# A fused convolution and SiLU MLP: first step as one whole chunk, second chunk by DMA transpose, output sums beside their own step

## The chip, the cores and the metric

The kernel runs on one core of one Trainium2 chip. The metric is device time in microseconds (us). A timed run and the profiled span differ by about 1.5 us (696.66 and 695.1 us for the kernel before); decompositions below use the span. In the profile, PE is the matmul engine (TensorE) and PEld its weight loads, DVE is VectorE, ACT is ScalarE, POOL is GpSimd and SP is the queue that issues most DMAs.

## The reference, cut to what matters

```python
def _attn_ref(x, weight):                    # x: 8 x 4096 x 192, weight: 8 heads x 7 taps
    w = exp(weight - max); w = w / sum(w)    # softmax over the 7 taps
    # causal depthwise convolution: out[s] = sum_k w[head, k] * x[s - 6 + k]
    ...
def _moe_ref(x, w_in, w_out, beta):          # 32768 x 192 -> 2048 -> 192
    h = x @ w_in
    g = h * sigmoid(beta * h)
    return (g @ w_out).astype(np.float32)
```

## The kernel before

Tokens are worked in chunks of 512, for two halves of the batch at once. A step takes one chunk through 16 groups. Group `u` does six input matmuls (`hidden`: 64 rows, 512 columns, two of them at a time on the two halves of the rows) and one activation of 128x1024, and beside them 16 output matmuls (`output`, 64 rows, 192 columns) of the **previous** step. Meanwhile VectorE convolves a later chunk by 21 "taps" (7 taps times 3 slices of the 192 channels), and evicts four output accumulators.

The first chunk is different: its convolution is done on PE with diagonal matrices, in two halves of 256 tokens, so that the first input matmul can start early. The second chunk comes in by a casting DMA and is transposed on PE. All later chunks are cast into HBM by GpSimd DMAs and then transposed by a DMA on the SP queue.

```python
    steps = [(0, 0, TOK // 2), (0, TOK // 2, TOK // 2)]        # chunk 0 in two halves
    steps += [(ch, 0, TOK) for ch in range(1, N_CH)]
    ...
    def xpose(ch):                                             # DMA transpose, SP queue
        nc.sync.dma_start_transpose(new_xt(ch)[:, :, r0:], xd[r0:].rearrange(...))
    ...
            if fc == NF - 1 and (b == 1 or single):            # eviction: copy, then add
                    nc.vector.tensor_copy(dst, po[:, 0, cols])
                nc.vector.tensor_tensor(dst, po[:, 1, cols], dst, ALU.add)
                store(s, h, q, n_q, osb)
    ...
    pops = {1: 12, 2: 26}
    for s in range(N_ST + 1):
        if s + 2 < N_ST:
            queue.extend(conv_ops(s + 2))      # step s + 2 reads chunk s + 1
        for u in range(NF):
            if s < N_ST:
                hidden(s, u)
            if s > 0:
                output(s - 1, u)               # the step before
            ...
            for _ in range(pops_u):            # 24 taps a step
                if queue:
                    queue.popleft()()
            if u == 0 and s + 4 < N_CH:
                cast(s + 4)
            if u == 1 and s + 2 < N_CH:
                xpose(s + 2)                   # convolved one step later
```

## Time and profile before

| Kernel before | us |
|---|---|
| time, median of 3 runs | 696.66 |
| profiled span | 695.1 |
| start of the first activation | 11.84 |
| last activation of chunk 1 ends | 53.5 |
| each of the next 30 steps (the first of them 20.63) | 20.92 |
| from the last activation to the end of the span | 14.3 |

The step times here and below are read from the trace: the end of the 16th activation of a step, less that of the step before.

The page of the kernel before, its fourth part (the chain of waits that ended last, by engine and by line):

```profile
PE 96%; DVE 3%; ACT 0%; issue 0%
PE po L442 48%; PE ph L395 46%; DVE ct L378 2%; PE ph L256 0%; DVE w_in_s L172 0%; DVE ct L376 0%; PE ph L205 0%; PE po L209 0%; PE po L243 0%; ACT g L402 0%; PE po L256 0%; DVE xt L346 0%; DVE osb L457 0%; DVE ct L327 0%; ACT xt_145 L269 0%
```

Nearly the whole chain is PE at work: L395 are the input and L442 the output matmuls. The groups of the same page (busy time, mean ns of one, then idle time of that engine just before them and who ended it):

```profile
L402 ACT ACTIVATE g<-ph,beta 128x1024 bf16<-128x1024 f32 (+1 forms) x528 | 572.7, 1090 | 96.7 <-PE ph L395 92.6
...
L378 DVE SCALAR_TENSOR_TENSOR ct<-xt,cw,ct 128x512 bf16<-128x512 bf16 x558 | 379.4, 745 | 0.0
...
L456 DVE COPY osb<-po 128x384 f32<-128x384 f32 x127 | 70.8, 558 | 126.9 <-PE po L442 120.7
L457 DVE TENSOR_TENSOR osb<-po,osb 128x384 f32<-128x384 f32 x129 | 71.5, 555 | 6.0 <-ACT osb L454 1.6
...
L376 DVE TENSOR_SCALAR ct<-xt,cw 128x512 bf16<-128x512 bf16 x93 | 29.5, 372 | 0.0
```

The copies (L456) stand 120.7 us in all for PE to finish an accumulator: VectorE is ahead of PE. And the first tap of a chunk (L376), which needs the DMA transpose, never waits: its idle time is 0.0. VectorE and the SP queue of the kernel before around 305 us (start, us, engine, line, operation, count, and in brackets the idle time before it):

```profile
303.79 0.56 DVE L456 COPY osb<-po 128x384 f32<-128x384 f32 x1 [0.77 <-PE po L442]
304.38 0.56 DVE L457 TENSOR_TENSOR osb<-po,osb 128x384 f32<-128x384 f32 x1
304.85 0.87 DVE L376 TENSOR_SCALAR ct<-xt,cw 128x512 bf16<-128x512 bf16 x3
```

```profile
304.96 0.37 SPq L417 DMA_DIRECT2D out_dram<-osb  x1
305.44 1.48 SPq L104 DMA_TRANSPOSE xt<-xd  x1
```

A copy and an add take 1.06 us from the start of the copy to the start of the next tap. The transpose is issued behind the store, at 305.44, while VectorE has been convolving another chunk, already in place, since 304.85. That the transpose lands some 5 us later hurts nobody.

### The profile page before, as it was taken

How to read it: one execution, taken by the hardware profiler on the slowest of the kernel's cores; microseconds unless marked ns; L12 is line 12 of the kernel's file. 1: busy time of each engine (PE TensorE's matmuls, PEld its weight loads, DVE VectorE, ACT ScalarE, POOL GpSimd, SP SyncE). 2: the span in 40 equal slices, each digit the busy share in tenths (PEclk: the TensorE clock that was granted, in tenths of full speed). 3: DMA queues.
4: the chain of work that ended last, by engine and by line, in shares of the span. 5: the costliest groups of instructions: out<-in, count | busy, mean ns of one | idle time of the engine just before them, and what ended most of it. 6: DMA issues, size and time to landing. Idle time of an engine off the chain costs nothing.

```text
span 695.1 us, 24865 instructions
## 1 busy us (share of the span) xinstructions
PE 687.6 (99%) x11467; PEld 526.6 (76%) x11467; DVE 551.4 (79%) x938; ACT 580.0 (83%) x546; POOL 70.0 (10%) x83
## 2 busy tenths in 40 slices
PE   9999999999999999999999999999999999999997
PEld 6867777777777777777777777777777777777777
DVE  5999998998777987777987777987778987777222
ACT  6898888888888888888888888888888888888881
POOL 7934455000000000000000000000000000000000
PEclk9999999999999999999999999999999999999999
DMA  9999999922232022222023222032222122211012
GB/s 193 144 159 159 168 177 171 123 63 70 54 65 71 27 68 72 47 70 70 26 71 70 49 70 70 25 71 70 48 71 55 40 70 71 48 48 48 25 48 70
DMA packets 181497, 54.57 MB, mean 79 GB/s; under 512 B 146432, under 2 KB 181072, under 8 KB 181392
## 3 DMA queue, kind: packets, MB, share of 16 engines
q0 software_dynamic: 98048, 14.89, 29.8%
q1 hardware_dynamic: 83296, 38.09, 23.9%
q8 instruction: 89, 1.46, 0.9%
q14 instruction: 16, 0.13, 0.1%
q10 hardware_dynamic: 48, 0.01, 0.0%
HBM read 28.98 MB, written 37.29 MB: 95 GB/s over the span
## 4 chain that ended last, share of the span: by engine, by line
PE 96%; DVE 3%; ACT 0%; issue 0%
PE po L442 48%; PE ph L395 46%; DVE ct L378 2%; PE ph L256 0%; DVE w_in_s L172 0%; DVE ct L376 0%; PE ph L205 0%; PE po L209 0%; PE po L243 0%; ACT g L402 0%; PE po L256 0%; DVE xt L346 0%; DVE osb L457 0%; DVE ct L327 0%; ACT xt_145 L269 0%
## 5 line engine op out<-in xcount | busy, mean ns | idle before, releaser
L402 ACT ACTIVATE g<-ph,beta 128x1024 bf16<-128x1024 f32 (+1 forms) x528 | 572.7, 1090 | 96.7 <-PE ph L395 92.6
L442 PEld LDWEIGHTS <-g 64*128 64x128 bf16 x8192 | 369.2, 94 | 101.9
L442 PE MATMUL po<-w_out_s,g 64*128 64x192 bf16 x8192 | 429.8, 243 | 0.0
L395 PE MATMUL ph<-ct,w_in_s 64*128 64x512 bf16 (+1 forms) x3168 | 426.2, 370 | 2.0 <-ACT g L402 1.1
L378 DVE SCALAR_TENSOR_TENSOR ct<-xt,cw,ct 128x512 bf16<-128x512 bf16 x558 | 379.4, 745 | 0.0
L395 PEld LDWEIGHTS <-w_in_s 64*128 64x128 bf16 x3168 | 162.5, 94 | 56.4 <-issue 2.9
L456 DVE COPY osb<-po 128x384 f32<-128x384 f32 x127 | 70.8, 558 | 126.9 <-PE po L442 120.7
L457 DVE TENSOR_TENSOR osb<-po,osb 128x384 f32<-128x384 f32 x129 | 71.5, 555 | 6.0 <-ACT osb L454 1.6
L95 POOL DMA_DIRECT2D xd<-in_x_dram x60 | 54.4, 909 | 46.1 <-DMA xd<-in_x_dram 42.3
L376 DVE TENSOR_SCALAR ct<-xt,cw 128x512 bf16<-128x512 bf16 x93 | 29.5, 372 | 0.0
L454 ACT COPY osb<-po 128x192 f32<-128x192 f32 x2 | 0.6, 320 | 9.9 <-PE po L442 9.9
L352 POOL TENSOR_TENSOR w_out_s<-w_out_raw,beta_r 128x768 bf16<-128x768 f32 x4 | 6.2, 1568 | 2.5 <-DMA w_out_raw<-in_moe_w_out_dram 2.5
L205 PE MATMUL ph<-zeros 128*128 128x512 bf16 x7 | 3.5, 623 | 1.3 <-DVE warm L129 1.3
L172 DVE COPY w_in_s<-w_in_s 64x1536 bf16<-64x1536 bf16 x4 | 4.4, 1121 | 0.1
L256 PE MATMUL po<-xt_145,diag 128*128 128x256 f32 x28 | 4.4, 296 | 0.0
L256 PEld LDWEIGHTS po<-xt_145,diag 128*128 128x128 f32 x28 | 3.6, 189 | 0.7 <-issue 0.6
L256 PEld LDWEIGHTS ph<-xt_145,diag 128*128 128x128 f32 x14 | 3.1, 327 | 0.6 <-ACT xt_145 L269 0.6
L256 PE MATMUL ph<-xt_145,diag 128*128 128x256 f32 x14 | 3.4, 427 | 0.1
L185 POOL DMA_DIRECT2D w_out_raw<-in_moe_w_out_dram x4 | 3.1, 771 | 0.3 <-DMA x1b<-in_x_dram 0.3
L295 ACT ACTIVATE ct<-po,rn 128x256 bf16<-128x256 f32 x1 | 0.5, 475 | 2.6 <-PE po L256 2.6
L165 POOL DMA_DIRECT2D w_in_s<-in_moe_w_in_dram x4 | 2.7, 669 | 0.0
L205 PEld LDWEIGHTS <-zeros 128*128 128x128 bf16 x7 | 0.8, 126 | 2.3 <-DVE warm L129 1.3
(51 smaller groups left out, 28.1 us busy)
## 6 DMA issues: line engine op xcount, KB each, us to landing
out_dram<-osb SPq DMA_DIRECT2D x60, 384.0 KB, 3.1
xd<-in_x_dram POOLq DMA_DIRECT2D x54, 198.0 KB, 14.5
w_out_raw<-in_moe_w_out_dram POOLq DMA_DIRECT2D x4, 384.0 KB, 9.4
out_dram<-osb SPq DMA_DIRECT2D x7, 192.0 KB, 3.7
xd<-in_x_dram POOLq DMA_DIRECT2D x6, 192.0 KB, 13.7
x_83<-in_x_dram SPq DMA_DIRECT2D x4, 192.0 KB, 2.9
w_in_s<-in_moe_w_in_dram POOLq DMA_DIRECT2D x4, 192.0 KB, 7.7
xt<-xd SPq DMA_TRANSPOSE x30, 5.1
```

Of the source, the lines that this page charges most:

```text
L95: nc.gpsimd.dma_start(out=xd[r0:, :, h, :], in_=x_v[p, t0:t1, h, :].rearrange("t (c d) -> t c d", c=NG),)
L172: nc.vector.tensor_copy(w_in_s[DG : 2 * DG, :, cols], w_in_s[0:DG, :, cols])
L205: nc.tensor.matmul(pf[:, 0, :], zeros[:, 0:128], zeros, start=True, stop=True)
L256: nc.tensor.matmul(pv, diag[:, c, k, :], xt0[:, c, o : o + n], start=(k == 0), stop=(k == K - 1),)
L352: nc.gpsimd.tensor_tensor(w_out_s[:, c0 : c0 + n, :], w_out_raw[:, c0 : c0 + n, :], beta_r[:, c0 : c0 + n].unsqueeze(2).to_broadcast((128, ...
L376: nc.vector.tensor_scalar_mul(dst, src, scalar)
L378: nc.vector.scalar_tensor_tensor(out=dst, in0=src, scalar=scalar, in1=dst, op0=ALU.mult, op1=ALU.add)
L395: nc.tensor.matmul(ph[:, h, 0:n], w_in_s[rows, j, cols], cts[s][rows, j, 0:n], start=(j == 0), stop=(j == NG - 1),)
L402: nc.scalar.activation(gs[s][:, fc, :, 0:n], ph[:, :, 0:n], AF.Silu, scale=beta[:, fc : fc + 1])
L442: nc.tensor.matmul(po[:, r, b * D : (b + 1) * D], g[rows, fc, h, q * BLK : (q + 1) * BLK], w_out_s[rows, fc, :], start=(fc == 0), stop=(fc ...
L456: nc.vector.tensor_copy(dst, po[:, 0, cols])
L457: nc.vector.tensor_tensor(dst, po[:, 1, cols], dst, ALU.add)
```

## The change

Its intent: spend the lead-in better. The whole first chunk is convolved by diagonals at N=512 and becomes one full step; the second chunk comes in by a DMA transpose instead of 48 small PE transposes (one third of its convolution is still done on PE, beside step 0); and the output sums of a step start in two accumulators while that step's own activations still run, so that fewer are left over at the end. Evictions become one reduce over the two halves of an accumulator. The core of the diff:

```diff
-    steps = [(0, 0, TOK // 2), (0, TOK // 2, TOK // 2)]
-    steps += [(ch, 0, TOK) for ch in range(1, N_CH)]
-    N_ST = len(steps)
+    N_ST = N_CH
 ... (psum_o with two buffers becomes psum_a and psum_b with one each)
+    cast(1)
+    for i in range(1, NW):
+        load_w_in(i)
+    cast(2)
+    cast(3)
+    xpose(1)                                   # on the SP queue ...
+    for i in range(1, NW):
+        load_w_out(i)                          # ... ahead of these weights
 ...
+    for c in range(NG):                        # chunk 0 whole: 21 matmuls at N=512
+        for k in range(K):
+            diag_tap(c, k, xt0[:, c], pv)
 ...
+                nc.vector.tensor_reduce(       # eviction
+                    dst,
+                    self.po[:, :, 0 : nb * D].rearrange("p r n -> p n r"),
+                    axis=mybir.AxisListType.X,
+                    op=ALU.add,
+                )
 ...
+    LAG = 2                                    # own step's sums, two groups behind
 ...
+    first_work = {
+        1: lambda: (copy_w_in(1), scale_w_out(1)),
 ...
+            output(s, u, 8, "a" if s == 0 and u <= CONV1[-1] else "ab")
 ...
             if u == 1 and s + 2 < N_CH:
                 xpose(s + 2)
+                queue.extend(conv_ops(s + 2, 0))   # step s + 2 now reads chunk s + 2
```

## The prediction

> **What bounds it now.** PE. The chain of waits that ended last is 96% PE; the page shows PE busy 99%, granted clock full. In the timeline a full step (16 times 6 input and 16 output matmuls) repeats every 16 x 1.308 = 20.92 us. VectorE was busy 89% from 100 to 200. So 32 x 20.92 = 669 us is GEMM at full rate; the other 26 us of the 695.1 us span are lead-in (first input matmul at 10.88), first half steps, and tail (last input matmul 679.5).
>
> **What the change does to start and end.**
> - Lead-in grows: 21 diagonal matmuls at N=512 instead of 256 (157 ns each when warm, 240 before). I estimate the first activation near 15 us instead of 11.84.
> - Step 0 becomes one full step, bound by activations: 16 x 1.09 = 17.4 us, with outputs hidden beside it. DMA transposes land 10.4 us after issue here, so chunk 1 arrives near its use (18 to 20 us). Step 0 ends at 33 to 34 us.
> - Then 31 steps x 20.92 = 648.6. The order of instructions shows 144 output matmuls after the last hidden one instead of 256: 5.9 us instead of 10.5. With 4.1 us of last eviction and store: 692, a gain of 3 us if nothing else changed.
> - Evictions: copy + add (1.06 us a pair) become one reduce over 768 PSUM elements. A 128x768 PSUM read by tensor_tensor took 0.94 us; the Trainium skill, "VectorE: DVE Perf Modes", section on the perf-mode tier table, gives tensor_reduce 1x only. I expect about 0.93 us.
>
> **What I think decides it: a new loop through VectorE.** Before, the taps run in a step read a chunk transposed one step earlier. Now chunk s+2 is transposed and convolved in the same step. The transpose stands on the SP queue behind the two stores of the pair of reduces at the start of the step, and the taps follow it. A backlog of 19 taps hides this at first, but 24 are popped and 21 pushed per step: 16, 13, 10, 7, 4, 1, 0. From step 8 the order of VectorE is: two reduces, 3 taps, reduce, 6 taps, reduce, 12 taps, two reduces. The cycle: store and queue 0.5 + transpose to landing 5.0 (quiet stage) + 3 first taps at 0.29 + 18 taps at 0.675 back to back + 4 reduces at about 0.92 + waits 0.2 = about 22.5 us, against PE's 20.92. PE then waits for the delayed reduce at the start of each step: 22 steps (8 to 29) x 1.6 = 35 us, plus 6 us in steps 4 to 7 (contended landings). Steps 30 and 31 convolve nothing: full rate.
>
> **Predicted:** span about 732, time 734 us; 8 in 10 between 712 and 752. Faster 0.03, same 0.11, slower 0.86.
>
> **Signs.** Right: VectorE idle about 5 us per step at the first tap, released by the transpose's landing; PE waiting 1 to 2.5 us per step on the reduce at the first output matmul of the second input group; step period about 22.5 us from step 8, 20.9 in the last two; first steps near 21; tail shorter by 4 us; first activation near 15.
>
> **What would make it wrong.** A reduce costlier than 1.1 us (two PSUM banks, strided) adds 4x the excess per step; landings under 3.5 us would close the loop within PE's time and leave about 692 to 697.

## The result

| | before | after |
|---|---|---|
| time, median of 4 runs each (us) | 696.66 | 720.38 |
| ratio, 95% interval | | 1.0342 (1.0328 to 1.0357) |
| profiled span | 695.1 | 719.7 |
| start of the first activation | 11.84 | 16.95 |
| from there to the end of chunk 1's last activation | 41.7 | 51.2 (30.15 + 21.08) |
| the 30 steps after that | 627.3 | 641.0 |
| from the last activation to the end of the span | 14.3 | 10.5 |

A ratio is the mean time of one kernel's runs over that of the other's of the same rounds, so it is not quite the ratio of the medians quoted. Executions over 1.5% slower than the fastest of the same kernel are left out of the means. The change makes the kernel 3.4% slower. The rows of the table add up: +5.1, +9.6, +13.7 and -3.8 make the 24.6 us by which the span grew.

The page of the changed kernel, the same part as shown for before:

```profile
PE 43%; DVE 27%; DMA 24%; issue 4%; POOL 1%; SPq 1%; ACT 0%; POOLq 0%
PE ph L363 20%; DVE ct L347 18%; DMA xd<-in_x_dram 14%; PE pa L393 12%; PE pb L393 10%; DMA xt<-xd 9%; DVE osb L412 7%; DVE ct L345 1%; POOL xd L104 1%; SPq L420 1%; ACT g L371 0%; POOL sel L158 0%; POOL sel L167 0%; POOL sel L156 0%; DVE osb L410 0%
```

The chain is no longer PE alone: 27% of it is VectorE and 24% DMA, among them 9% for the transposes (`DMA xt<-xd`). A chain that goes from DMA to VectorE to PE and round again is what a loop of waits looks like on a page. Not every wait on the chain is a cost: most of the 14% for the casts (`DMA xd<-in_x_dram`) lies between 46 and 113 us, and the steps there take 21.1 to 21.2 us, no more than later steps without any stall. The groups of the page:

```profile
L347 DVE SCALAR_TENSOR_TENSOR ct<-xt,cw,ct 128x512 bf16<-128x512 bf16 x552 | 371.7, 745 | 0.0
L393 PE MATMUL pa<-w_out_s,g 64*128 64x192 bf16 x4128 | 240.5, 243 | 9.3 <-DVE osb L412 7.5
...
L345 DVE TENSOR_SCALAR ct<-xt,cw 128x512 bf16<-128x512 bf16 x92 | 27.5, 351 | 119.2 <-DMA xt<-xd 119.2
L412 DVE TENSOR_REDUCE osb<-pa 128x384 f32<-128x768 f32 x64 | 61.0, 954 | 42.0 <-PE pa L393 41.9
...
L256 PE MATMUL pb<-xt,diag 128*128 128x512 f32 x7 | 4.1, 582 | 8.2 <-DVE xt L327 8.2
...
L291 DVE TENSOR_TENSOR w_out_s<-w_out_raw,beta_r 128x768 bf16<-128x768 f32 x4 | 3.8, 952 | 8.3 <-DMA w_out_raw<-in_moe_w_out_dram 8.3
```

The first taps (L345) now stand 119.2 us for the transposes, where before they stood for nothing; output matmuls stand 7.5 us for the reduces; and the diagonal matmul of chunk 1 (L256 into `pb`) stands 8.2 us, VectorE 8.3 us for output weights (L291). These are three different places. First the regular steps, VectorE of the changed kernel over one cycle:

```profile
303.83 0.95 DVE L412 TENSOR_REDUCE osb<-pa 128x384 f32<-128x768 f32 x1
304.70 0.95 DVE L412 TENSOR_REDUCE osb<-pb 128x384 f32<-128x768 f32 x1
310.80 0.88 DVE L345 TENSOR_SCALAR ct<-xt,cw 128x512 bf16<-128x512 bf16 x3 [5.15 <-DMA xt<-xd]
311.59 0.95 DVE L412 TENSOR_REDUCE osb<-pa 128x384 f32<-128x768 f32 x1
312.46 4.06 DVE L347 SCALAR_TENSOR_TENSOR ct<-xt,cw,ct 128x512 bf16<-128x512 bf16 x6
316.43 0.95 DVE L412 TENSOR_REDUCE osb<-pb 128x384 f32<-128x768 f32 x1
317.30 8.03 DVE L347 SCALAR_TENSOR_TENSOR ct<-xt,cw,ct 128x512 bf16<-128x512 bf16 x12
325.25 0.95 DVE L412 TENSOR_REDUCE osb<-pa 128x384 f32<-128x768 f32 x1
326.12 0.94 DVE L412 TENSOR_REDUCE osb<-pb 128x384 f32<-128x768 f32 x1
```

its SP queue in the same stretch:

```profile
304.81 1.24 SPq L420 DMA_DIRECT2D out_dram<-osb  x2
306.15 1.50 SPq L113 DMA_TRANSPOSE xt<-xd  x1
```

and PE at the start of it:

```profile
303.31 0.83 PE L363 MATMUL ph<-ct,w_in_s 64*128 64x512 bf16 x6
304.84 0.83 PE L393 MATMUL pa<-w_out_s,g 64*128 64x192 bf16 x16 [0.69 <-DVE osb L412]
```

After the second reduce VectorE has nothing to do until 310.80, 5.15 us, because the transpose of the chunk it has to convolve in this step was issued only at 306.15, behind the two stores of the two reduces. VectorE then does its taps and reduces without a pause, the next pair of reduces comes late, and PE stands for the first reduce of the pair (0.69 us here, 0.32 us at the end of this cycle). From the second reduce of one pair to that of the next the cycle is 0.95 + 5.15 + 0.79 + 0.87 + 3.97 + 0.87 + 7.95 + 0.87 = 21.42 us, against 20.92 us that PE needs for a step.

That explains steps of 21.4 to 22 us. But the trace also holds many steps in which PE shows no idle time over 0.15 us and which still take 21.17 us, not 20.92. The times of the activations put the extra 0.247 us (1.555 instead of 1.308 us) into one place, from the second to the third activation of the step. PE and VectorE there, in a step of 21.17 us:

```profile
367.02 0.51 PE L393 MATMUL pa<-w_out_s,g 64*128 64x192 bf16 x8
367.36 0.51 PE L393 MATMUL pb<-w_out_s,g 64*128 64x192 bf16 x8
367.69 0.83 PE L363 MATMUL ph<-ct,w_in_s 64*128 64x512 bf16 x6
368.58 0.84 PE L393 MATMUL pa<-w_out_s,g 64*128 64x192 bf16 x16
```

```profile
367.57 0.96 DVE L412 TENSOR_REDUCE osb<-pa 128x384 f32<-128x768 f32 x1 [0.38 <-PE pa L393]
```

Accumulator `pa` gets its last matmuls at 367.02, `pb` its last at 367.36: both end in the same group. The next output matmuls need `pa` again at once. PE has only the eight matmuls of `pb` and the next six input matmuls to do in between, 0.33 + 0.65 = 0.98 us, while the reduce starts at 367.57 and ends at 368.53, and `pa` is used again at 368.58: the next group starts 0.24 us after the input matmuls that precede it would have let it (367.69 + 0.65 = 368.34). Every step pays this, a new handoff wait that the prediction's arithmetic left out.

The third place is step 0. The windows view of the changed kernel (busy us of each engine in each stretch, number of instructions, then granted clock PEclk, DMA share, GB/s):

```profile
20.00:25.00 5.00, 0.94 (x10) 0.22 (x5) 0.00 (x0) 2.12 (x3) 1.45 (x3) 0.85 1.55 181
25.00:30.00 5.00, 0.88 (x5) 0.44 (x7) 2.21 (x4) 0.00 (x0) 1.35 (x2) 0.50 1.50 230
30.00:35.00 5.00, 5.00 (x32) 1.89 (x28) 4.93 (x8) 2.09 (x2) 0.80 (x1) 0.62 1.83 147
```

PE stands from 20.97 to 29.12 us, VectorE from 19.45 to 27.76 and ScalarE from 22.12 to 31.67; for 5.6 us all three stand at once. When PE returns, the granted clock is 0.50, and it stays there until 33.8 us (0.62 is the mean of the third stretch). What they stood for, in the timeline of the same kernel:

```profile
14.77 2.91 SPq L113 DMA_TRANSPOSE xt<-xd  x1
...
17.74 4.08 SPq L132 DMA_DIRECT2D w_out_raw<-in_moe_w_out_dram  x3
...
27.76 0.96 DVE L291 TENSOR_TENSOR w_out_s<-w_out_raw,beta_r 128x768 bf16<-128x768 f32 x1 [8.32 <-DMA w_out_raw<-in_moe_w_out_dram]
28.64 0.43 DVE L327 CAST xt<-xt 128x528 fp32r<-128x528 bf16 x1
...
29.12 0.80 PE L256 MATMUL pb<-xt,diag 128*128 128x512 f32 x1 [8.15 <-DVE xt L327]
```

Chunk 1 was cast into HBM by 14.70 us, its transpose issued at 14.77 and landed at 24.34. The output weights stand behind it on the SP queue, were issued from 17.74 and the first of them landed at 27.74. VectorE, in order, has to scale these weights (L291) before it may copy chunk 1 (L327), and PE, in order, has the first diagonal matmul of chunk 1 (L256) ahead of the rest of step 0.

### The profile page after: what moved, and what is told of

It is laid out like the page before. It is cut to its first block, busy times and chain, and to the rows that moved or that the text cites. A ratio compares the mean times of both kernels' runs of the same rounds, so it can differ in the third digit from the quotient of the medians.

```text
span 719.7 us, 24619 instructions
## 1 busy us (share of the span) xinstructions
PE 696.2 (97%) x11325; PEld 521.7 (72%) x11325; DVE 522.7 (73%) x807; ACT 578.7 (80%) x532; POOL 60.4 (8%) x74
## 4 chain that ended last, share of the span: by engine, by line
PE 43%; DVE 27%; DMA 24%; issue 4%; POOL 1%; SPq 1%; ACT 0%; POOLq 0%
PE ph L363 20%; DVE ct L347 18%; DMA xd<-in_x_dram 14%; PE pa L393 12%; PE pb L393 10%; DMA xt<-xd 9%; DVE osb L412 7%; DVE ct L345 1%; POOL xd L104 1%; SPq L420 1%; ACT g L371 0%; POOL sel L158 0%; POOL sel L167 0%; POOL sel L156 0%; DVE osb L410 0%
## 5 line engine op out<-in xcount | busy, mean ns | idle before, releaser
L371 ACT ACTIVATE g<-ph,beta 128x1024 bf16<-128x1024 f32 x512 | 570.2, 1115 | 122.5 <-PE ph L363 118.5
L393 PEld LDWEIGHTS <-g 64*128 64x128 bf16 x8192 | 368.0, 94 | 121.1 <-issue 20.5
L363 PE MATMUL ph<-ct,w_in_s 64*128 64x512 bf16 x3072 | 424.5, 377 | 0.3 <-ACT g L371 0.2
L347 DVE SCALAR_TENSOR_TENSOR ct<-xt,cw,ct 128x512 bf16<-128x512 bf16 x552 | 371.7, 745 | 0.0
L393 PE MATMUL pa<-w_out_s,g 64*128 64x192 bf16 x4128 | 240.5, 243 | 9.3 <-DVE osb L412 7.5
L393 PE MATMUL pb<-w_out_s,g 64*128 64x192 bf16 x4064 | 224.5, 243 | 0.0
L345 DVE TENSOR_SCALAR ct<-xt,cw 128x512 bf16<-128x512 bf16 x92 | 27.5, 351 | 119.2 <-DMA xt<-xd 119.2
L412 DVE TENSOR_REDUCE osb<-pa 128x384 f32<-128x768 f32 x64 | 61.0, 954 | 42.0 <-PE pa L393 41.9
L412 DVE TENSOR_REDUCE osb<-pb 128x384 f32<-128x768 f32 x63 | 59.8, 950 | 10.9 <-PE pb L393 10.9
L256 PE MATMUL pb<-xt,diag 128*128 128x512 f32 x7 | 4.1, 582 | 8.2 <-DVE xt L327 8.2
L256 PEld LDWEIGHTS pb<-xt,diag 128*128 128x128 f32 x7 | 1.5, 215 | 11.9 <-DVE xt L327 8.6
L291 DVE TENSOR_TENSOR w_out_s<-w_out_raw,beta_r 128x768 bf16<-128x768 f32 x4 | 3.8, 952 | 8.3 <-DMA w_out_raw<-in_moe_w_out_dram 8.3
L213 PE MATMUL ph<-zeros 128*128 128x512 bf16 (+2 forms) x11 | 4.7, 501 | 1.3 <-DVE warm L152 1.3
L256 PE MATMUL ph<-xt,diag 128*128 128x512 f32 x14 | 5.7, 594 | 0.0
L256 PEld LDWEIGHTS ph<-xt,diag 128*128 128x128 f32 x14 | 4.3, 313 | 1.3 <-ACT xt L273 0.2
## 6 DMA issues: line engine op xcount, KB each, us to landing
w_in_s<-in_moe_w_in_dram POOLq DMA_DIRECT2D x3, 192.0 KB, 11.1
```

The costliest lines, as they stand in the source:

```text
L213: nc.tensor.matmul(pf[:, 0, 0:cols], zeros[:, 0:128], zeros[:, 0:cols], start=True, stop=True)
L256: nc.tensor.matmul(pv, diag[:, c, k, :], xt[:, o : o + TOK], start=(k == 0), stop=(k == K - 1))
L291: nc.vector.tensor_tensor(w_out_s[:, fcs, :], w_out_raw[:, fcs, :], beta_r[:, fcs].unsqueeze(2).to_broadcast((128, NQ, D)), ALU.mult,)
L345: nc.vector.tensor_scalar_mul(dst, src, scalar)
L347: nc.vector.scalar_tensor_tensor(out=dst, in0=src, scalar=scalar, in1=dst, op0=ALU.mult, op1=ALU.add)
L363: nc.tensor.matmul(ph[:, h, :], w_in_s[rows, j, fc * 128 : (fc + 1) * 128], cts[s][rows, j, :], start=(j == 0), stop=(j == NG - 1),)
```

## The experiments

The theory: (a) the late transpose closes a loop through SP queue, DMA and VectorE; (b) the two accumulators that end together cost 0.25 us a step; (c) step 0 stands for chunk 1's way through HBM and for the order of the weights; (d) the lead-in is longer. The main rivals: VectorE's wait at the taps is slack and costs nothing; the evictions are off the path; step 0 is held by VectorE's own work or by DMA bandwidth. The first four kernels change the regular steps, the others start from the third of them and change step 0. All gave correct results. "Ratio" is against the kernel before in the same rounds; the changed kernel has 1.0342.

### Early transpose

```diff
             if u == 1 and s + 2 < N_CH:
-                xpose(s + 2)
+                if s == 0:
+                    xpose(2)
                 queue.extend(conv_ops(s + 2, 0))
+            if u == 9 and s + 3 < N_CH:
+                xpose(s + 3)
```

> The changed kernel with one edit: the transpose of a chunk is issued in the middle (group 9) of the step before the one that convolves it, so it no longer stands behind the two stores that follow the pair of reduces at the start of the step. Loop theory: VectorE's wait at the first tap (about 5 us a step in the changed kernel, 119 us in all) falls to near 0, the steps that took 21.5 to 22 us fall to 21.17 us, and the time falls by about 5 to 6 us, to about 715 us. The other 0.25 us a step (the handoff of accumulators) and the stall in step 0 stay. Rival (the long steps are only the reduce of the two accumulators that end together; VectorE's wait is slack): the waits at the taps go, but the time stays within 1 us of 720.

Measured: 714.53 us (713.28 to 715.90), ratio 1.0253 (1.0239 to 1.0267). Every step from 2 to 31 takes 21.17 us in the trace. The waits view has no wait for the transpose any more; the longest one is now

```profile
DVE osb L412 <- PE pa L393: 142.5, 59, 9.2
```

and the chain of its page, 43% PE in the changed kernel, reads

```profile
PE 91%; DVE 5%; DMA 3%; POOL 0%; issue 0%; SPq 0%; ACT 0%; POOLq 0%
```

so VectorE is ahead of PE again. The loop (a) is real and cost about 6 us (0.9% of 696.7). Most of VectorE's 119 us of waiting was slack, though: the rival was right about that share.

### Stagger

```diff
-            output(s, u, 8, "a" if s == 0 and u <= CONV1[-1] else "ab")
+            output(s, u, 2 if (s, u) == (0, NF - 1) else 8, "a" if ...)
```

Two pairs instead of up to eight, once, in the last group of step 0: from then on `pb` ends one group after `pa`.

> The changed kernel with one edit: in the last group of step 0 two pairs of output matmuls are done instead of up to eight, once. By the order of instructions this shifts all later steps so that the second accumulator ends one group after the first, and the next output group no longer needs the first one's reduce at once: from the end of the first accumulator to its next use PE has 1.31 us of other work instead of 0.98. Handoff theory: the 0.25 us that every step pays at its second group goes, up to 30 x 0.25 = 7.5 us, but the loop through the transpose (mean cycle about 21.2 to 21.4 us) now sets the step, so only part shows: 714 to 719 us, with steps uneven around 21.1 to 21.4. If the 0.25 us had another cause (changing between two accumulators, the longer order), nothing changes at the second group.

Measured: 717.31 us (714.83 to 718.64), ratio 1.0287 (1.0268 to 1.0305). Steps that the loop does not hold take 20.92 us now (steps 2, 3 and 20 in the trace, among others), others up to 21.96. Handoff (b) is confirmed, and as expected the loop keeps part of the gain.

### Both

> Both edits: early transpose and stagger. If the loop and the handoff are the two causes of the 13.5 us by which 31 steps exceed 31 x 20.92, steps 1 to 31 come back to 20.92 us each and the time falls to about 707 us (13 us less than the changed kernel), more than the sum of the two edits alone if each hides the other. What is left over the kernel before is then step 0 and the lead-in (about 15 us) less the shorter tail (4 us). If the steps stay above 21.0, a third cause is at work.

Measured: 706.95 us (706.41 to 707.55), ratio 1.0142 (1.0129 to 1.0156). All steps from 2 to 31 take 20.92 us (step 1 takes 20.83). In the changed kernel and in this one, the wait of output matmuls for a reduce (total us, times, longest) reads

```profile
PE pa L393 <- DVE osb L412: 7.5, 13, 0.9
```

```profile
PE pa L393 <- DVE osb L412: 0.4, 1, 0.4
```

The two causes together are worth 13.4 us (720.38 - 706.95), and the regular steps are back at what they took before the change. Alone the edits gave 5.9 and 3.1 us: each cause hid part of the other. With the handoff out of the way the loop costs 717.31 - 706.95 = 10.4 us.

### Copy and add instead of the reduce

The changed kernel with the eviction of before (copy of one half, add of the other) in place of the reduce.

> The changed kernel with the eviction of before: a copy and an add (1.06 us of VectorE in the kernel before) in place of one reduce (0.87 us back to back). If handoff and loop set the steps as I think, both grow: the handoff by 0.15 to 0.25 us a step, the loop's cycle by 4 x 0.19 = 0.76 us, so steps of about 21.9 to 22.2 us and a time of about 738 us (721 + 23 x 0.75). If evictions are off the critical path, no change: 720.

Measured: 735.6 us (734.76 to 736.40), ratio 1.0553 (1.0539 to 1.0567). The time is 2.4 us under the one expected. The cheapest steps take 21.37 us, 0.20 more than with the reduce, as expected of the handoff; nine of the 31 steps take 22.2 to 22.4. So the reduce was a good part of the change: without it the change would have cost 15 us more. In the kernel before, the same eviction stood in steps of 20.92 us, with VectorE ahead of PE.

### Weights first

Base from here on: both edits (706.95 us). The loads of output weights 1 to 3 are issued ahead of the first transpose.

```diff
-    load_w_out(0)
+    for i in range(NW):
+        load_w_out(i)
 ...
     xpose(1)
-    for i in range(1, NW):
-        load_w_out(i)
```

> Base is the kernel with early transpose and stagger (706.95 us), where only step 0 and the lead-in are left. Edit: the loads of output weights 1 to 3 stand before the first transpose on the SP queue instead of behind it. In the changed kernel the first transpose lands at 24.3 us and the weights at 27.7 us, and VectorE, which scales weights 1 before it copies chunk 1, stands until 27.8. Theory (the order of weights behind the transpose costs the last 4 us of the stall, chunk 1's own way of cast, HBM and transpose the rest): PE resumes when the transpose lands; the loads now compete with the cast, so it lands at 25 to 27 us; gain 1 to 3 us, time 704 to 706. If the weights alone were the cause, the stall (8.6 us) would nearly vanish: 697 to 699 us.

Measured: 708.78 us (707.00 to 710.81), ratio 1.0184 (1.0159 to 1.0209). A miss: no gain, rather a loss of 2 to 3 us (the base was measured in other rounds). The weights now landed at 18.4 to 23.0 us, but the cast of chunk 1 landed at 17.5 us (14.7 in the changed kernel) and its transpose at 28.3 (24.3). With one load moved ahead, the other landed later. The order of the weights alone was not the cause.

### Chunk 1 transposed on PE

On top of weights first, chunk 1 is brought in as before the change:

```diff
-    cast(1)
+    x1b = setup.tile([128, NB, 2, D], BF16)
+    for h in range(2):
+        nc.gpsimd.dma_start(out=x1b[:, :, h, :], in_=x_v[0, TOK : 2 * TOK, h, :]...)
 ...
-    xpose(1)
 ...
+        2: second_xt,            # group 2 of step 0: 48 transposes on PE, one copy
```

> Base as e5, with its edit, and chunk 1 brought in as before the change: loaded by a casting DMA straight to SBUF and transposed on PE (48 small transposes, about 2 us of PE in group 2 of step 0), no DMA transpose for it. Theory: chunk 1 then lands by about 13 us and is ready at about 19 us, so group 4 of step 0 does not wait, the clock is not throttled down, step 0 takes about 18 to 20 us instead of 30, and the time falls by about 10 us to 696 to 698 us, the time of the kernel before. Rival: if step 0 is held by VectorE's own work (weights scaled and copied, 16 taps) or by DMA bandwidth as a whole, step 0 stays above 24 us and the time above 701 us.

Measured: 697.67 us (697.39 to 698.14), ratio 1.0020 (1.0005 to 1.0035). Step 0 takes 20.5 us instead of 30.1, PE is idle in it for about 0.4 us, and the windows view shows the clock at 1.00 throughout where it had fallen to 0.50:

```profile
20.00:25.00 5.00, 4.86 (x47) 2.10 (x43) 4.90 (x9) 4.17 (x4) 1.79 (x2) 1.00 2.33 165
25.00:30.00 5.00, 5.00 (x44) 2.11 (x42) 3.66 (x6) 4.07 (x5) 2.73 (x4) 1.00 2.14 157
30.00:35.00 5.00, 5.00 (x88) 3.58 (x84) 5.00 (x8) 4.19 (x5) 1.80 (x2) 1.00 1.62 158
```

So neither VectorE's own work (4.90 of 5 us busy at first, but ahead of need) nor DMA bandwidth as a whole held step 0; chunk 1's way did, the cast to HBM and then a transpose that took 9.6 us to land. The run undoes the cast and the transpose together, so it does not tell their shares. It is worth 11.1 us against weights first, measured in the same rounds, and 9.3 us against the base of other rounds (8.5 by the ratios). Beside the 13.4 us of the regular steps this is the other large cost of the change.

### Scale weights later

Base: both edits, without weights first. Only the order on VectorE is changed: weights 1 are scaled in group 5 of step 0 instead of group 1.

```diff
-        1: lambda: (copy_w_in(1), scale_w_out(1)),
-        5: lambda: copy_w_in(2),
+        1: lambda: copy_w_in(1),
+        5: lambda: (scale_w_out(1), copy_w_in(2)),
```

> Base as e5 but without its edit: only the order on VectorE is changed, output weights 1 are scaled in group 5 of step 0 instead of group 1, behind the copy of chunk 1. Chunk 1 is then copied when its transpose lands (24.3 us) and PE resumes near 24.8 instead of 29.1; it then waits again at group 6 for the scaled weights (landed 27.7, scaled about 28.7). Expect the first wait shorter by 4 us, 1 to 2 us of it lost again at group 6: time 703.5 to 705 us. If VectorE's order did not matter: 707.

Measured: 703.34 us (703.14 to 706.32), ratio 1.0111 (1.0091 to 1.0132). Step 0 takes 27.5 us instead of 30.1; the time between the ends of the activations of groups 4 and 5 is 7.5 us instead of 10.9. The first activation, which the edit does not touch, also came 1.8 us earlier in the profiled run (14.95 against 16.73), so the 3.6 us between the two times are not all gain of the edit. By the trace of step 0, of the stall about 3 us belonged to the order on VectorE and the rest to chunk 1's landing.

### More fill

Base: chunk 1 on PE (697.67 us). The dummy matmuls of the lead-in fill more of PE's gaps.

> Base is the PE-transpose kernel of the run before (697.67 us). Edit: the dummy matmuls of the lead-in fill more of PE's gaps (6 instead of 5 at the start, widths 384 to 512 instead of 128 to 384 later). In the runs so far the clock reached full speed between 9.2 and 13.3 us in the same lead-in, and a diagonal matmul over 512 columns took 0.43 us before that and 0.23 after. Theory: with fewer gaps the clock rises by about 10 us always, the first activation comes near 15 us instead of 16.6, and the time is about 696 us, level with the kernel before (696.5). Rival: the lead-in is held by the arrival of the last x block and of the first weights; then no change: 697.7.

Measured: 698.14 us (697.40 to 698.65), ratio 1.0022 (1.0010 to 1.0035): no change. The clock did rise at 9.4 us in the profiled run (12.0 in that of the base), yet the first activation came at 16.5 us. VectorE stood until 12.98 us for the first input weights, which the changed lead-in loads twice in float32, and took 1.75 us to convert them. The rival held: in that run the weights, not the clock, set the end of the lead-in.

### Outputs after their step

Base: chunk 1 on PE. The third part of the change is undone alone.

```diff
-    LAG = 2
+    LAG = NF + 1
```

> Base is the PE-transpose kernel (697.67 us). Edit: a step's output sums wait until its own step is over, as in the kernel before, so that the third part of the change is undone alone. By the order of instructions 256 instead of 144 output matmuls are left after the last input matmul: 4.6 us more at the end. Step 0 loses its 112 output matmuls (4.6 us of PE work) and would come back to 17 to 18 us from 20.5, since activations (1.11 us a group) and the diagonal matmuls then set it. Steps stay at 20.92. So I expect a net loss of only 1.5 to 2.5 us: 699 to 700 us. If the shorter tail were a full gain: 702 us. If it were only moved: 697.7.

Measured: 698.86 us (698.51 to 699.59), ratio 1.0037 (1.0023 to 1.0050), against 1.0020 of its base: about 1.2 us slower. The ratios are of different rounds and their intervals overlap, so the traces must carry it: the end after the last activation grows from 10.9 to 14.1 us, step 0 shrinks from 20.5 to 18.3. So of the 3.2 us that the shorter tail seems to bring, about 1 us is a net gain. The rest was moved into step 0, where PE was not as idle as the idea needs. This holds for the kernel whose step 0 no longer stalls; in the changed kernel it was not tested.

### First weights as before

Base: more fill. The first input weights come again by one casting DMA and a copy of 64 rows.

> Base is the more-fill kernel (698.14 us), whose clock rose at 9.4 us but whose first activation still came at 16.5, since VectorE waited until 13.0 us for the first input weights and then took 1.75 us to convert them. Edit: those weights come as before the change, by one casting DMA at the head of the GpSimd queue (landed 8.5 us in the kernel before) and a copy of 64 rows (0.69 us), not by two plain loads of the full width. Theory (the second limit of the lead-in is these weights): no wait for them, first activation at 14.3 to 15 us, time 696 to 696.7 us, level with the kernel before. Rival (the lead-in is PE work now): 16 us or more and no change, 698.1.

Measured: 697.45 us (697.19 to 697.75), ratio 1.0006 (0.9993 to 1.0020). The first activation came at 14.8 us, as the theory said, 1.7 us earlier. Not all of this is due to the weights: in this run the clock rose at 4.7 us and in that of the base at 9.4, and the first 14 diagonal matmuls took 3.50 us instead of 4.10, so I estimate that 0.6 us of the gain belongs to the clock. Of the 1.7 us, 0.7 came back in step 0 (21.8 us), whose group 4 took 2.6 us, since VectorE finished chunk 1's copies only at 20.6 us. The best version is level with the kernel before. It does not beat it.

## Why the prediction was right or wrong

**Direction and mechanism: right.** The loop was named from the order of instructions before any run, and it is there: VectorE idle 5 us a step released by the transpose, in every step from 8 to 29. Early transpose removed it and its cost. The sign for PE was too large, though: it waits for a reduce 0.9 us at most, not 1 to 2.5.

**The size of the loop: wrong, by a factor of four to seven.** The prediction put 41 us on it (35 + 6); early transpose gained 5.9 us, and 10.4 with the handoff out of the way. The term that was mis-sized is the cycle, 22.5 us predicted against 21.42 measured in the cycle shown and 21.40 as the mean of steps 8 to 29. Part by part: queue and landing 5.5 against 5.15 us (median landing 4.7 against the 5.0 taken from before); first taps 0.87 against 0.79; 18 taps 12.15 against 11.92; four reduces 3.68 against 3.56; waits 0.2 against none. The three large parts are off by 2 to 7 per cent, but the cost is the difference of two nearly equal numbers, cycle less PE's step, so an error of 1 us in 22 turned 0.5 us into 1.6. The extra cost in steps 4 to 7 was also too high: these four steps together took 0.6 us more than 4 x 21.17.

**What PE needs for a step: wrong.** The prediction compared the loop with 20.92 us, and said so of the last two steps too, which took 21.5 and 21.17 us. The changed order needs 21.17, since `pa` and `pb` end in one group. The prediction saw that they end together, but put this wait down to the loop; the two edits against early transpose alone (714.53 to 706.95 us) show that it is a cost of its own, about 7.6 us over the run.

**Step 0: wrong.** Predicted 17.4 us, ending at 33 to 34 us; measured 30.15, ending at 47.1. The failing step was "chunk 1 arrives near its use (18 to 20 us)": the transpose landed at 24.3, and VectorE's order added until 28.6. The prediction took only the landing time of a transpose from the trace; it did not add up the queue (cast landed 14.7, issue 14.77) nor look at what stands ahead of the copy on VectorE. Chunk 1 on PE brought step 0 to 20.5 us. The idle PE then also lost its clock. The Trainium skill, "TensorE: Matmul & The Clock Gate", section "Part 1: The HAM clock gate", describes this: a busy window releases the throttle and an idle one brings it back. The trace agrees: granted clock 0.50 from 25 to 30 us, and back to 1.00 from 35 us on.

**The lead-in: too short by 2 us.** 15 us expected, 16.95 measured. In that run the clock rose at 13.3 us. The twelve diagonal matmuls begun before then took 0.43 us each (the first 0.57, the last 0.28), the later ones 0.23. The prediction named no time for the rise; in the kernel before it came at 9.9 us. But in the run of both edits the clock rose at 9.3 us and the first activation still came at 16.7, held by the first weights. So there are two limits, and which one binds differs from run to run.

**The tail: right in size.** 3.8 us shorter, 4 predicted. Outputs after their step showed, on the kernel with chunk 1 on PE, that only about 1 us of it is a net gain.

**The reduce: right.** 0.95 us, 0.87 back to back, where 0.93 was expected from a read of 768 elements. The skill's "VectorE: DVE Perf Modes", section on the perf-mode tier table, gives `tensor_reduce` the slowest mode only; at 0.95 us it still beats a copy and an add (1.06).

So the errors offset each other: the loop cost 35 us less than predicted, step 0, handoff and lead-in some 22 us more, and the measured time lies 14 us below the central value, inside the range. That the total came so near is luck; what was foreseen is the direction and the loop, not its weight.

## What to carry to other kernels

Before moving a load nearer to its use, write down in which queue it stands and what stands ahead of it: here a transpose behind two stores closed a loop through DMA, VectorE and PE, although VectorE was busy for only 74 of the 100 us from 300 to 400 us. Two accumulators that finish together are one buffer, not two; shifting one of them by a group, once, freed 0.25 us in every step. And when a cost is the small difference of two long cycles, give it a wide range.

## What the Trainium skill lacked or had wrong

- "TensorE: Matmul & The Clock Gate" gives the length of the idle window after which the clock falls, but not how much of that window has to be idle. In the changed kernel the clock fell to 0.50 at 23.5 us, 2.6 us after PE had stopped (20.97), and rose at 33.8 us, 4.7 us after PE had resumed (29.12). The first group after the stall took 2.35 us where the next ones took 1.35.
- "VectorE: DVE Perf Modes" calls `tensor_reduce` the slowest operation and advises to consider restructuring. Here, adding two halves of a PSUM accumulator of 128x768, one reduce (0.95 us, 0.87 back to back) was cheaper than the copy and add that avoid it (1.06 us), and the kernel with the reduce was 15 us faster (720.38 against 735.6 us).
- I found no page with the time from issue to landing of a DMA transpose of this size (528 tokens by 384 channels, bf16) under load: 3.7 to 5.8 us in the quiet stages of the two kernels, 9.6 to 13.8 us in the changed kernel while the casts of later chunks ran. The casts alone do not settle it: one transpose of the kernel before, issued at 22.0 us among casts, landed after 4.8 us.
